# Hashed attention and an MLP on one core: the later queries of batch 0's first head group are hashed in a column-tiled matmul and their bits spread through DRAM, with the order of instructions rewritten

## The chip, the core and the metric

The kernel runs on 1 core of one Trainium2 chip. The metric is the device time in microseconds (us) of one execution; smaller is better. TensorE is called PE (its weight loads PEld), VectorE DVE, ScalarE ACT, GpSimd POOL and SyncE SP, as in the profile. SP's work is to issue most of the DMAs.

## What is computed

Four batches, 8 heads, 768 positions, head width 64. Queries and keys are hashed to 6 bits by the signs of a projection, and a query sees only the keys with the same 6 bits. The 8 heads side by side make rows of 512 for a normalised two-layer network with 2048 hidden units, which is added to its input.

```python
q_bits = (np.einsum('bhsd,dk->bhsk', q, proj) > 0).astype(np.int64)
k_bits = (np.einsum('bhsd,dk->bhsk', k, proj) > 0).astype(np.int64)
mask = q_bucket[:, :, :, None] == k_bucket[:, :, None, :]
scores = np.where(mask, scale * np.matmul(q, k.transpose(0, 1, 3, 2)), -1000000000.0)
attn = softmax(scores)                       # over the keys
x = heads_side_by_side(np.matmul(attn, v))   # (4, 768, 512)
xn = (x - mu) / np.sqrt(var + 1e-06) * g_ln
return x + np.maximum(xn @ w_ch1, 0.0) @ w_ch2
```

(The lines are shortened; `q_bucket` and `k_bucket` are the numbers that the bits spell.)

## The kernel before

**Tiling.** A batch's heads are two groups `g` of 4. Four heads lie in four strips of 32 partitions, so that a score matmul works on one strip and four of them fill the PE array. A unit `u` is 256 queries; there are 3 units in a batch and 12 in all. A step `s` is one unit, one group and one third `kp` of the keys: `s = 6u + 3g + kp`, 72 steps.

**A step.** `S` computes the scores of 4 heads: for each, three matmuls that add into one PSUM tile, the first on the bits (`G`, 6 partitions of a strip, values of plus or minus one half), the other two on the two halves of the head width. The bits' share is so scaled that a query and a key with unequal bits get a negligible weight. `E` is the exponential on ACT, in two halves of 2 heads. `A` multiplies by the values, with a column of ones for the row sums. `na` adds a very small multiple of the plain value sums, `nb` divides, `nc` and `ce` normalise the row, `rs` makes the inverse deviation, and `fl` transposes the row block by a DMA; for unit 0 PE transposes instead (`ft`) and DVE or ACT copies (`fc`). `F` and `R` are the first layer and its ReLU in eight parts, `D` the second layer in quarters for each half of the unit, `Z` the final addition, `O` the output's DMA.

**Inputs.** q and k come in as `X` tiles (`lx` in thirds for batch 0, `LX` whole for the others; four buffers, so a load waits for the last reader of the tile whose place it takes). DVE turns them in blocks of 32 (`tn` for batch 0, into three `tp` buffers; `tu` for the others), and `ca` or `CA` cast them to bf16 on ACT, DVE or POOL. `lv` and `cv` load and cast the values, `sv` and `sw` make batch 0's value sums with a matmul by ones. `lw1` and `lw2` load the network's weights in eight pieces by way of POOL's queue, and `lg` loads the row `g_ln` for all partitions.

**The hash.** For batch 0 there is one `ha` for each group, each of q and k and each third: two fp32 matmuls of 128 x 256, with a projection `pfull` that has the 6 columns of strip i at column 32i. So the six results of strip i land on the partitions where `G` wants them, and `bi` turns them to bits and writes them there. For batches 1 to 3, `hm` hashes a whole group in 16 instructions on 32 columns each, with `p32` (strip i's 6 columns at column 8i); four chunks of positions use the four column groups of the array at the same time. `bt` makes the bits in a tile `B`, and 16 small DMAs (`mo`) copy them to `G`, one for each chunk and strip.

**The order.** Nothing is scheduled at run time. A string `ORDER` holds words such as `ha.t.0.1.2`: the function, the engine (v DVE, a ACT, p POOL, s SP, t PE), and its numbers. Words are emitted in this order, and each engine runs its own words strictly in that order, waiting at each until its inputs and buffers are ready. For `tn`, `ca`, `ha` and `bi` the numbers are group, 0 for q or 1 for k, and third; for `S`, the step; for `F` and `R`, unit and part. SP issues its DMAs in order as well, all from one queue; the weights' DMAs have another.

The words of the front run over the first 60 us: hash, first ten steps, unit 0's network, and the loads of batch 1. Score steps 0 to 5 read queries 0 to 255 (third 0 of q); steps 6 to 11 read queries 256 to 511, steps 12 to 17 the rest. So the bits of group 0's thirds 1 and 2, which the change touches, are first read in step 6, 7 or 8. PSUM has the tags `scA` and `scB` (a half step's scores each), `acc` (the sums of `A`; lent to scores in steps 0 to 5), `f1` and `f2`.

Of the kernel before, what the change touches and what calls it, by code (L numbers as in the profile page):

```python
# [9 lines left out]
BF16 = mybir.dt.bfloat16  # L10
# [7 lines left out]
mem.v on.p.1 on.p.0 lp.a pf.v lx.s.0.1.1.3 tn.v.0.1.2 ca.p.0.1.2 tn.v.0.1.1 lx.s.0.0.0.1 tn.v.0.0.0 ca.a.0.0.0  # L18
ca.a.0.1.1 lx.s.1.0.0.1 warm.t ha.t.0.1.2 bi.v.0.1.2 tn.v.1.0.0 ca.p.1.0.0 ha.t.0.0.0 bi.v.0.0.0 lx.s.0.1.0.1
tn.v.0.1.0 ca.a.0.1.0 ha.t.1.0.0 bi.v.1.0.0 pmem.p p32.p S.t.2.2 E.a.2.1 E.a.2.0 lv.s.0.0.4 cv.p.0.0.2 ha.t.0.1.1  # L20
bi.v.0.1.1 ha.t.0.1.0 lx.s.1.1.0.3 tn.v.1.1.2 ca.p.1.1.2 S.t.1.2 E.a.1.1 E.a.1.0 lx.s.1.0.1.3 ha.t.1.1.2 bi.v.0.1.0
S.t.0.2 E.a.0.0 E.a.0.1 lg.s tn.v.1.1.1 ha.t.1.1.1 ca.p.1.1.1 bi.v.1.1.2 S.t.5.2 E.a.5.1 tn.v.1.1.0 ca.p.1.1.0
ha.t.1.1.0 cv.p.0.0.0 A.t.1.2 A.t.0.2 bi.v.1.1.1 lw1.p.0 E.a.5.0 S.t.4.2 E.a.4.1 lw1.p.1 lx.s.0.0.1.3 tn.v.0.0.2
tn.v.0.0.1 ha.t.0.0.1 ca.v.0.0.1 lw2.p.1 E.a.4.0 bi.v.1.1.0 sv.t.0 LX.s.1.0.1 tu.v.1.0.1.3 tu.v.1.0.1.1 tu.v.1.0.1.2
lw1.p.3 tu.v.1.0.1.0 lw2.p.0 CA.p.1.0.1.1 tn.v.1.0.2 A.t.2.2 bi.v.0.0.1 S.t.6.2 E.a.6.0 E.a.6.1 ha.t.1.0.2 sw.v.0
na.v.0.0 nb.v.0.0 S.t.3.2 nc.v.0.0 E.a.3.1 bi.v.1.0.2 ha.t.0.0.2 lv.s.0.4.4 cv.p.0.4.0 cv.p.0.4.2 sv.t.4 LX.s.1.0.0
tu.v.1.0.0.0 tu.v.1.0.0.2 lv.s.1.4.1 S.t.8.2 E.a.3.0 A.t.3.2 E.a.8.0 A.t.5.2 E.a.8.1 A.t.4.2 ca.v.1.0.2 tn.v.1.0.1
ca.v.1.0.1 bi.v.0.0.2 ha.t.1.0.1 S.t.7.2 E.a.7.1 E.a.7.0 LX.s.1.1.1 lw1.p.2 sw.v.4 na.v.0.1 nb.v.0.1 A.t.8.2
nc.v.0.1 A.t.6.2 ce.v.0.0 bi.v.1.0.1 ft.t.0.0 fc.a.0.0 S.t.10.2 E.a.10.0 E.a.10.1 ce.v.0.1 ft.t.0.1 rs.p.0
tu.v.1.0.0.1 A.t.7.2 fc.v.0.1 F.t.0.0 R.a.0.0 CA.v.1.0.0.0 LX.s.1.1.0 S.t.11.2 E.a.11.1 E.a.11.0 lw2.p.2  # L30
tu.v.1.0.0.3 CA.a.1.0.0.1 hm.t.1.0 bt.v.1.0 mo.s.1.0.3.0 mo.s.1.0.0.0 mo.s.1.0.2.3 mo.s.1.0.0.3 mo.s.1.0.1.2
mo.s.1.0.0.1 mo.s.1.0.1.3 mo.s.1.0.3.3 mo.s.1.0.0.2 F.t.0.7 R.v.0.7 lw2.p.3 S.t.9.2 E.a.9.1 CA.p.1.0.1.0 F.t.0.6
F.t.0.3 na.v.1.0 nb.v.1.0 A.t.10.2 ca.v.0.0.2 E.a.9.0 S.t.14.2 E.a.14.1 tu.v.1.1.0.3 A.t.9.2 R.v.0.6 mo.s.1.0.2.2
E.a.14.0 nc.v.1.0 R.v.0.3 lv.s.1.0.0 A.t.11.2 na.v.1.1 F.t.0.4 R.a.0.4 LX.s.2.1.1 F.t.0.1 R.a.0.1 S.t.13.2 E.a.13.0
E.a.13.1 nb.v.1.1 A.t.14.2 nc.v.1.1 ce.v.1.0 ce.v.1.1 fl.s.1.1 fl.s.1.0 F.t.0.5 R.a.0.5 tu.v.1.1.0.0 lv.s.1.4.2
F.t.0.2 R.a.0.2 LX.s.2.0.0 lv.s.1.4.3 lv.s.1.0.3 tu.v.1.1.0.1 mo.s.1.0.1.1 mo.s.1.0.1.0 mo.s.1.0.2.1 tu.v.1.1.1.3
S.t.12.2 E.a.12.1 E.a.12.0 tu.v.1.1.1.0 tu.v.1.1.0.2 CA.a.1.1.0.1 mo.s.1.0.2.0 lv.s.1.0.1 mo.s.1.0.3.1 LX.s.2.0.1
D.t.0.0.0 D.t.0.0.1 D.t.0.0.2 D.t.0.0.3 S.t.16.2 E.a.16.0 E.a.16.1 mo.s.1.0.3.2 tu.v.1.1.1.1 F.t.1.7 R.v.1.7
A.t.13.2 A.t.12.2 na.v.2.0 F.t.1.2 R.a.1.2 S.t.17.2 E.a.17.1 E.a.17.0 tu.v.1.1.1.2 CA.p.1.1.1.1 hm.t.1.1 Z.v.0.0
D.t.0.1.0 bt.v.1.1 mo.s.1.1.3.2 mo.s.1.1.3.0 mo.s.1.1.2.1 mo.s.1.1.1.1 mo.s.1.1.0.1 mo.s.1.1.0.0 mo.s.1.1.1.2  # L40
mo.s.1.1.3.1 F.t.1.0 R.a.1.0 S.t.15.2 E.a.15.0 E.a.15.1 rs.p.1 nb.v.2.0 nc.v.2.0 A.t.16.2 A.t.17.2 mo.s.1.1.0.3
# [78 lines left out]
def kernel(  # L120
# [15 lines left out]
    nc = tc.nc  # L136
    P = 128
# [453 lines left out]
```

## Time and profile before

| | |
|---|---|
| time, median of 3 runs (lowest to highest) | 304.76 us (303.95 to 304.84) |
| the profiled execution: time, span | 304.76 us, 303.0 us |
| mean granted PE clock in it | 0.998 |
| PE busy in the span | 292.2 us |
| ACT, DVE, POOL busy | 194.6, 169.7, 72.0 us |
| first score matmul, first `F` of unit 0, end of the last weight load on PE | 9.03, 35.67, 298.89 us |

The span is the time from the first to the last instruction of the execution. The profile's groups have, after the bar, the busy time of all, the mean ns of one, and the idle time of the engine before them with what ended it. fp32 matmuls have two records for each instruction, so one `ha` (two instructions) shows as four. In the chain and the timelines the first column is the start in us, the second the duration.

### The profile page before, as it was taken

Reading aid. Unit: us, or ns where it says so; the run is one execution under the profiler, and the core shown is the slowest. Engines: PE = TensorE matmul, PEld = TensorE weight load, DVE = VectorE, ACT = ScalarE, POOL = GpSimd, SP = SyncE. Lnnn points to the kernel's source line nnn. Section 1 sums busy time; section 2 is a strip of 40 time slices with the busy share of each in tenths; the row PEclk is TensorE's granted clock in tenths of the full one; section 3 lists DMA queues with packets and bytes.
Section 4 is the critical chain, followed back from the end, with each engine's and each line's share of the span. In section 5 each row is a group of like instructions: output and inputs, shape, how many; then the busy total and the mean of one; then the engine's idle time right before and its main releaser. Section 6 shows DMA issues by size and latency. Waiting matters only on the chain.

```text
span 303.0 us, 9838 instructions
## 1 busy us (share of the span) xinstructions
PE 292.2 (96%) x4319; PEld 204.8 (68%) x4360; DVE 169.7 (56%) x348; ACT 194.6 (64%) x215; POOL 72.0 (24%) x112
## 2 busy tenths in 40 slices
PE   8999899999999999999999999999999999999994
PEld 7667676676666667676667677776657667685673
DVE  4678878378258527766345767555217446266012
ACT  2977789667667788686567676557666767561320
POOL 2792500211771005041600520911000101001000
PEclk9999999999999999999999999999999999999999
DMA  6999996937255265516306100310502102403122
GB/s 202 381 340 306 209 205 142 268 111 169 47 147 122 61 217 167 94 74 160 73 2 175 38 8 8 75 42 19 89 2 71 37 2 19 105 4 74 30 71 69
DMA packets 30426, 33.58 MB, mean 111 GB/s; under 512 B 15536, under 2 KB 27056, under 8 KB 30384
## 3 DMA queue, kind: packets, MB, share of 16 engines
q1 hardware_dynamic: 25792, 28.50, 35.1%
q0 software_dynamic: 4224, 4.19, 8.4%
q8 instruction: 34, 0.56, 0.8%
q10 hardware_dynamic: 368, 0.26, 0.3%
q14 instruction: 8, 0.07, 0.1%
HBM read 27.53 MB, written 6.29 MB: 112 GB/s over the span
## 4 chain that ended last, share of the span: by engine, by line
PE 80%; DMA 6%; SPq 6%; DVE 3%; issue 2%; ACT 1%; DVEq 0%; ACTq 0%
PE f L511 26%; PE sc L443 15%; PE acc L458 10%; DMA X<-in_q_dram 4%; SPq L420 3%; PE hp L408 3%; DMA xnT<-xc 3%; ACT E L449 1%; SPq L294 1%; PE f_100None L527 1%; PE f_101None L527 1%; PE f L527 1%; PE f_11None L527 1%; PE f_51None L527 1%; PE f_80None L527 1%
## 5 line engine op out<-in xcount | busy, mean ns | idle before, releaser
L449 ACT ACTIVATE E<-sc,bias_sb 128x1024 bf16<-128x1024 f32 x144 | 153.1, 1111 | 49.5 <-PE sc L443 48.3
L511 PE MATMUL f<-xnT,w_sb 128*128 128x256 bf16 x768 | 99.3, 273 | 0.8 <-DMA xnT<-xc 0.7
L511 PEld LDWEIGHTS <-w_sb 128*128 128x128 bf16 x768 | 70.9, 98 | 23.5 <-issue 7.9
L519 ACT ACTIVATE hb<-f 128x512 bf16<-128x512 f32 x57 | 33.9, 597 | 44.6 <-PE f L511 44.5
L527 PEld LDWEIGHTS <-hb 128*128 128x128 bf16 x400 | 37.7, 98 | 34.5 <-issue 2.7
L521 DVE TENSOR_SCALAR hb<-f 128x512 bf16<-128x512 f32 x39 | 26.9, 690 | 46.7 <-PE f L511 46.4
L443 PE MATMUL sc<-qb,kb 32*128 32x256 bf16 x1152 | 52.2, 267 | 0.0
L458 PEld LDWEIGHTS <-E 128*128 128x128 bf16 x1152 | 40.0, 98 | 6.5 <-issue 3.8
L458 PE MATMUL acc<-vaug,E 128*128 128x65 bf16 x1152 | 43.4, 194 | 0.1
L443 PE MATMUL sc<-G 6*128 6x256 bf16 x576 | 41.7, 273 | 0.9 <-DVE G L249 0.3
L489 POOL TENSOR_SCALAR rs<-mv 128x2 f32<-128x2 f32 x12 | 7.1, 595 | 104.6 <-DVE mv L483 104.3
L443 PEld LDWEIGHTS <-kb 32*128 32x128 bf16 x1152 | 30.2, 93 | 1.6
L443 PEld LDWEIGHTS <-G 6*128 6x128 bf16 x576 | 15.2, 91 | 18.8 <-issue 15.6
L246 DVE STREAM_TRANSPOSE T<-X 128x384 f32<-128x384 f32 x48 | 24.8, 554 | 3.4 <-PE hp L408 1.4
L469 DVE SCALAR_TENSOR_TENSOR acc<-vsB,acc 128x520 f32<-128x520 f32 x24 | 16.8, 701 | 15.3 <-PE acc L458 15.0
L356 POOL TENSOR_TENSOR t<-vn 128x256 f32<-128x256 f32 x18 | 12.9, 727 | 35.0 <-DMA out_dram<-x 18.0
L346 POOL CAST vaug<-vn 128x768 bf16<-128x768 f32 x16 | 13.1, 831 | 25.9 <-DMA G<-B 12.7
L484 DVE SCALAR_TENSOR_TENSOR xc<-x,mv,gB 128x512 bf16<-128x512 f32 x24 | 18.6, 776 | 0.8
L480 DVE BATCH_NORM_STATS2 st<-x 128x6 f32<-128x256 f32 x48 | 18.0, 417 | 0.7
L476 DVE TENSOR_TENSOR x<-acc,rc 128x512 f32<-128x512 f32 x24 | 16.6, 691 | 0.8
L257 POOL CAST kb<-T 128x768 bf16<-128x768 f32 x10 | 8.4, 842 | 30.2 <-DVE T L246 30.2
L315 PE MATMUL hf<-tp,pfull 128*128 128x256 f32 x48 | 13.2, 401 | 0.6 <-DVE tp L246 0.5
(98 smaller groups left out, 223.8 us busy)
## 6 DMA issues: line engine op xcount, KB each, us to landing
out_dram<-x SPq DMA_DIRECT2D x44, 128.0 KB
X<-in_k_dram SPq DMA_DIRECT2D x7, 768.0 KB
X<-in_q_dram SPq DMA_DIRECT2D x6, 768.0 KB
vn<-in_v_dram SPq DMA_DIRECT2D x24, 192.0 KB
w_sb<-in_moe_w_ch_dram POOLq DMA_DIRECT2D x8, 512.0 KB, 16.5
vn<-in_v_dram SPq DMA_DIRECT2D x2, 768.0 KB
G<-B SPq DMA_DIRECT2D x96, 4.5 KB
X<-in_q_dram SPq DMA_DIRECT2D x2, 512.0 KB
```

The source lines that it names most:

```text
L246: nc.vector.transpose(d[:, j], s[:, j, kj0 : kj0 + n])
L443: nc.tensor.matmul(sc(s, i // 2)[:, i % 2, 256 * kk : 256 * kk + 256], lh, rh, start=(rep == 0), stop=(rep == 2), skip_group_check=True,)
L449: nc.scalar.activation(E(s)[:, heads(h)], sc(s, h), AF.Exp, scale=EXP_SCALE, bias=bias_sb)
L458: nc.tensor.matmul(acc[:, qt, (D + 1) * i : (D + 1) * (i + 1)], E(s)[:, i, 256 * kk + P * qt : 256 * kk + P * qt + P], vaug(u // 3)[:, 4 * ...
L469: nc.vector.scalar_tensor_tensor(acc, vs, EPS_ROW, acc, op0=AOP.mult, op1=AOP.add)
L476: nc.vector.tensor_tensor(xo, a[:, :, :, 0:D], rc.to_broadcast([P, 2, 4, D]), op=AOP.mult)
L480: nc.vector.bn_stats(stats(u)[:, qt, g], xt(u)[:, qt, 256 * g : 256 * g + 256])
L484: nc.vector.scalar_tensor_tensor(xc(u)[:, t], xt(u)[:, t], mv(u)[:, t, 0:1], gB, op0=AOP.subtract, op1=AOP.mult,)
L511: nc.tensor.matmul(f1[:, n].rearrange("p (t x) -> p t x", t=2), w1_sb[:, dt, P * nt : P * nt + P], xnT(u)[:, :, dt], start=(dt == 0), stop ...
L519: nc.scalar.activation(hb(u)[:, 2 * p : 2 * p + 2], f1, AF.Relu)
L521: eng.tensor_scalar_max(hb(u)[:, 2 * p : 2 * p + 2], f1, 0.0)
L527: nc.tensor.matmul(f2, hb(u)[:, nt, P * t : P * t + P], w2_sb[:, nt, half(h)], start=(nt == 0), stop=(nt == NNT - 1),)
```

## The change

`ha.t.0.0.1`, `ha.t.0.0.2` and their two `bi` go. In their place one `hq.t.0` hashes queries 256 to 767 of group 0 in 8 instructions on 32 columns and 128 positions each, four chunks in the four column groups, with `p32`. `bq` makes the bits in a tile of 128 x 128. `dw` writes this tile to a tensor in DRAM, and four `dr`, one for each strip, read it back into `G`. All five are DMAs from SP's queue; `dr` waits until `dw` has landed. The other hashes stay as they are.

The whole order is rewritten as well. In the front, the first load is third 0 of q instead of thirds 1 and 2 of k; `lg` stands behind the loads of batch 1's first tiles; `pmem` and `p32` come first on POOL; steps run 2, 1, 0, 5, 4, 3, 11, 10, 7, 6 instead of 2, 1, 0, 5, 4, 6, 3, 8, 7, 10; and the parts of `F` of each unit, the casts' engines and the DMAs stand in another sequence to the end of the kernel.

```diff
 ORDER = """
-mem.v on.p.1 on.p.0 lp.a pf.v lx.s.0.1.1.3 tn.v.0.1.2 ca.p.0.1.2 tn.v.0.1.1 lx.s.0.0.0.1 tn.v.0.0.0 ca.a.0.0.0
-ca.a.0.1.1 lx.s.1.0.0.1 warm.t ha.t.0.1.2 bi.v.0.1.2 tn.v.1.0.0 ca.p.1.0.0 ha.t.0.0.0 bi.v.0.0.0 lx.s.0.1.0.1
-tn.v.0.1.0 ca.a.0.1.0 ha.t.1.0.0 bi.v.1.0.0 pmem.p p32.p S.t.2.2 E.a.2.1 E.a.2.0 lv.s.0.0.4 cv.p.0.0.2 ha.t.0.1.1
-bi.v.0.1.1 ha.t.0.1.0 lx.s.1.1.0.3 tn.v.1.1.2 ca.p.1.1.2 S.t.1.2 E.a.1.1 E.a.1.0 lx.s.1.0.1.3 ha.t.1.1.2 bi.v.0.1.0
-S.t.0.2 E.a.0.0 E.a.0.1 lg.s tn.v.1.1.1 ha.t.1.1.1 ca.p.1.1.1 bi.v.1.1.2 S.t.5.2 E.a.5.1 tn.v.1.1.0 ca.p.1.1.0
-ha.t.1.1.0 cv.p.0.0.0 A.t.1.2 A.t.0.2 bi.v.1.1.1 lw1.p.0 E.a.5.0 S.t.4.2 E.a.4.1 lw1.p.1 lx.s.0.0.1.3 tn.v.0.0.2
-tn.v.0.0.1 ha.t.0.0.1 ca.v.0.0.1 lw2.p.1 E.a.4.0 bi.v.1.1.0 sv.t.0 LX.s.1.0.1 tu.v.1.0.1.3 tu.v.1.0.1.1 tu.v.1.0.1.2
-lw1.p.3 tu.v.1.0.1.0 lw2.p.0 CA.p.1.0.1.1 tn.v.1.0.2 A.t.2.2 bi.v.0.0.1 S.t.6.2 E.a.6.0 E.a.6.1 ha.t.1.0.2 sw.v.0
-na.v.0.0 nb.v.0.0 S.t.3.2 nc.v.0.0 E.a.3.1 bi.v.1.0.2 ha.t.0.0.2 lv.s.0.4.4 cv.p.0.4.0 cv.p.0.4.2 sv.t.4 LX.s.1.0.0
-tu.v.1.0.0.0 tu.v.1.0.0.2 lv.s.1.4.1 S.t.8.2 E.a.3.0 A.t.3.2 E.a.8.0 A.t.5.2 E.a.8.1 A.t.4.2 ca.v.1.0.2 tn.v.1.0.1
-ca.v.1.0.1 bi.v.0.0.2 ha.t.1.0.1 S.t.7.2 E.a.7.1 E.a.7.0 LX.s.1.1.1 lw1.p.2 sw.v.4 na.v.0.1 nb.v.0.1 A.t.8.2
...
-mo.s.1.0.0.1 mo.s.1.0.1.3 mo.s.1.0.3.3 mo.s.1.0.0.2 F.t.0.7 R.v.0.7 lw2.p.3 S.t.9.2 E.a.9.1 CA.p.1.0.1.0 F.t.0.6
-F.t.0.3 na.v.1.0 nb.v.1.0 A.t.10.2 ca.v.0.0.2 E.a.9.0 S.t.14.2 E.a.14.1 tu.v.1.1.0.3 A.t.9.2 R.v.0.6 mo.s.1.0.2.2
-E.a.14.0 nc.v.1.0 R.v.0.3 lv.s.1.0.0 A.t.11.2 na.v.1.1 F.t.0.4 R.a.0.4 LX.s.2.1.1 F.t.0.1 R.a.0.1 S.t.13.2 E.a.13.0
-E.a.13.1 nb.v.1.1 A.t.14.2 nc.v.1.1 ce.v.1.0 ce.v.1.1 fl.s.1.1 fl.s.1.0 F.t.0.5 R.a.0.5 tu.v.1.1.0.0 lv.s.1.4.2
-F.t.0.2 R.a.0.2 LX.s.2.0.0 lv.s.1.4.3 lv.s.1.0.3 tu.v.1.1.0.1 mo.s.1.0.1.1 mo.s.1.0.1.0 mo.s.1.0.2.1 tu.v.1.1.1.3
...
+on.p.0 mem.v warm.t pmem.p lp.a pf.v lx.s.0.0.0.1 tn.v.0.0.0 ca.a.0.0.0 ha.t.0.0.0 lx.s.0.1.1.3 tn.v.0.1.2
+ha.t.0.1.2 ca.a.0.1.2 tn.v.0.1.1 p32.p ca.p.0.1.1 bi.v.0.0.0 ha.t.0.1.1 on.p.2 lx.s.0.1.0.1 tn.v.0.1.0 ca.a.0.1.0
+bi.v.0.1.2 S.t.2.2 E.a.2.1 E.a.2.0 ha.t.0.1.0 bi.v.0.1.1 S.t.1.2 E.a.1.1 E.a.1.0 lx.s.1.0.0.1 tn.v.1.0.0 ca.v.1.0.0
+lx.s.1.1.0.3 tn.v.1.1.2 ha.t.1.1.2 tn.v.1.1.0 ca.p.1.1.2 ca.p.1.1.0 bi.v.0.1.0 ha.t.1.0.0 S.t.0.2 E.a.0.0 bi.v.1.1.2
+ha.t.1.1.0 bi.v.1.0.0 S.t.5.2 E.a.0.1 lv.s.0.0.4 cv.p.0.0.0 cv.p.0.0.2 lx.s.1.0.1.3 tn.v.1.0.1 ca.p.1.0.1 tn.v.1.1.1
+ca.p.1.1.1 ha.t.1.1.1 lx.s.0.0.1.3 tn.v.0.0.2 ca.p.0.0.2 bi.v.1.1.0 sv.t.0 E.a.5.1 A.t.1.2 A.t.0.2 A.t.2.2
+LX.s.1.0.0 tu.v.1.0.0.0 tn.v.0.0.1 bi.v.1.1.1 lw1.p.2 E.a.5.0 S.t.4.2 E.a.4.0 lv.s.0.4.4 cv.p.0.4.2 cv.p.0.4.0
+E.a.4.1 tu.v.1.0.0.1 sw.v.0 na.v.0.0 hq.t.0 nb.v.0.0 S.t.3.2 E.a.3.1 bq.v.0 ha.t.1.0.1 tn.v.1.0.2 ca.p.1.0.2
+tu.v.1.0.0.2 lw1.p.3 sv.t.4 LX.s.1.1.1 bi.v.1.0.1 S.t.11.2 nc.v.0.0 ca.p.0.0.1 E.a.3.0 A.t.3.2 A.t.4.2 A.t.5.2
+lw1.p.0 LX.s.1.0.1 tu.v.1.0.1.2 tu.v.1.0.1.3 lg.s E.a.11.0 E.a.11.1 S.t.10.2 E.a.10.1 E.a.10.0 lw2.p.1 sw.v.4
+na.v.0.1 nb.v.0.1 nc.v.0.1 ce.v.0.0 ce.v.0.1 rs.p.0 ha.t.1.0.2 bi.v.1.0.2 lw1.p.1 ft.t.0.0 fc.v.0.0 dw.s.0 dr.s.0.0
+dr.s.0.3 dr.s.0.1 dr.s.0.2 S.t.7.2 E.a.7.0 E.a.7.1 ft.t.0.1 fc.v.0.1 F.t.0.4 R.a.0.4 S.t.6.2 E.a.6.1 E.a.6.0
+tu.v.1.0.0.3 CA.a.1.0.0.1 tu.v.1.0.1.1 lw2.p.0 A.t.7.2 F.t.0.7 R.a.0.7 tu.v.1.0.1.0 hm.t.1.0 bt.v.1.0 mo.s.1.0.1.2
+mo.s.1.0.2.0 mo.s.1.0.3.2 CA.p.1.0.1.0 mo.s.1.0.2.2 mo.s.1.0.1.0 mo.s.1.0.1.1 mo.s.1.0.3.3 mo.s.1.0.2.3 S.t.8.2
+E.a.8.0 E.a.8.1 F.t.0.0 R.a.0.0 A.t.6.2 CA.p.1.0.1.1 tu.v.1.1.1.0 F.t.0.5 R.v.0.5 S.t.9.2 E.a.9.1 E.a.9.0
+mo.s.1.0.0.0 lv.s.1.4.3 lv.s.1.0.1 A.t.8.2 F.t.0.3 R.a.0.3 F.t.0.6 R.a.0.6 lw2.p.3 mo.s.1.0.0.3 mo.s.1.0.3.1 lw2.p.2
+mo.s.1.0.1.3 S.t.13.2 E.a.13.1 E.a.13.0 tu.v.1.1.1.3 LX.s.1.1.0 tu.v.1.1.1.2 na.v.1.0 nb.v.1.0 nc.v.1.0 A.t.9.2
+A.t.10.2 A.t.11.2 F.t.0.1 R.a.0.1 S.t.14.2 E.a.14.1 E.a.14.0 F.t.0.2 R.a.0.2 tu.v.1.1.1.1 na.v.1.1 nb.v.1.1 nc.v.1.1
+ce.v.1.1 A.t.13.2 fl.s.1.1 ce.v.1.0 fl.s.1.0 lv.s.1.4.1 D.t.0.0.0 LX.s.2.0.1 S.t.12.2 E.a.12.1 E.a.12.0 mo.s.1.0.2.1
...

+    def hq(eng, g):
+        hp = ps(f"hq{g}", [P, P], "f1")
+        for j in range(2):
+            for c in range(4):
+                nc.tensor.matmul(
+                    hp[32 * c : 32 * c + 32], p32[:, j], tp(g, 0, 1 + c // 2)[:, j, P * (c % 2) : P * (c % 2) + P],
+                    start=(j == 0), stop=(j == 1), skip_group_check=True,
+                )
+
     def Bq(g):
         return sb(f"Bq{g}", [P, P], BF16, "B", 2)
+
+    def bq(eng, g):
+        bits(Bq(g), made[f"hq{g}"])
+
+    def dw(eng, g):
+        made["hs", g] = dram.tile([4, 4, 8, P], BF16, name=f"hs{g}")
+        eng.dma_start(out=made["hs", g].rearrange("c i n w -> (c i n) w"), in_=Bq(g))
+
+    def dr(eng, g, i):
+        eng.dma_start(
+            out=Gt(0, g)[32 * i : 32 * i + NB, 0, 256:S].rearrange("n (c w) -> n c w", c=4),
+            in_=made["hs", g][:, i, :NB].rearrange("c n w -> n c w"),
+        )
```

## Prediction

> **What bounds the kernel now.** I read the page first: which engine is full, and the chain that ended last. The profiled execution took 304.76 us, its span 303.0 us; the 1.76 us around it I keep. 304.76 is also the median of the three runs. A kernel of this length can be told from no change at about 0.3%, 0.91 us.
>
> ```profile
> span 303.0 us, 9838 instructions
> PE 292.2 (96%) x4319; PEld 204.8 (68%) x4360; DVE 169.7 (56%) x348; ACT 194.6 (64%) x215; POOL 72.0 (24%) x112
> ...
> DMA  6999996937255265516306100310502102403122
> ...
> PE 80%; DMA 6%; SPq 6%; DVE 3%; issue 2%; ACT 1%; DVEq 0%; ACTq 0%
> ```
>
> PE is busy 96% and carries 80% of the chain, so work taken off PE is worth its time if PE then finds the next operands ready. The DMA row is full in its first seven slices (up to about 53 us): that is where the change puts its transfers. Next, the groups of the two hash forms and of the small loads in front of the scores:
>
> ```profile
> L315 PE MATMUL hf<-tp,pfull 128*128 128x256 f32 x48 | 13.2, 401 | 0.6 <-DVE tp L246 0.5
> L408 PE MATMUL hp<-T,p 128*32 128x192 f32 x192 | 9.0, 329 | 0.0
> L443 PEld LDWEIGHTS <-G 6*128 6x128 bf16 x576 | 15.2, 91 | 18.8 <-issue 15.6
> ```
>
> The first two give what is removed and the nearest relative of what is added. The third shows 15.6 us of "issue" ahead of the score loads: a score step (`S`) that follows an unsplit matmul starts late. In the timeline of PE, `F` lasts 0.79 us start to start, but 1.18 us with `S` behind it; `D` 0.76 and 1.17; `A` 0.49 and 0.69; `S` itself 0.77, `ha` 1.06, `hm` 1.44.
>
> Then the chain in order of time for the first 40 us, and SP's and POOL's timelines:
>
> ```profile
> 6.31 10.99 DMA X<-in_q_dram
> ...
> 17.40 1.44 DVE tp L246 x4
> ```
> ```profile
> 39.89 7.90 SPq L420 DMA_DIRECT2D G<-B  x10
> ```
> ```profile
> 16.98 1.79 POOL L330 DMA_DIRECT2D w_sb<-in_moe_w_ch_dram  x2
> ```
>
> The front is paced by the last piece of X (issued 6.31, used 17.40), because everything before it is in one queue; from there by DVE. The `G<-B` copies cost SP 0.79 us each. In the trace's packet records the first of these, issued 39.89, moves its first packet at 44.08, 4.2 us later, while the weight queue moves 200 packets of 1 KB per us; one issued near 47.1, when weights run out, starts at 48.4, after 1.3 us. The first weight load, issued 16.98, moves packets from 20.5.
>
> **The change, part by part.**
>
> Hash. `ha.0.0.1` and `ha.0.0.2` go: 2 x 1.06 = 2.12 us of PE. `hq` has 16 records of the column-tiled form with 128 columns; `hm` has 32 with 192 in 1.44 us. By count alone hq is 0.72, by count and columns 0.48; I take 0.60. Gain 1.5 us (1.4 to 1.64). DVE loses two bits steps of 0.41 and gains one of half their width, about 0.3: 0.5 us, at a place where DVE is full (3.79 and 3.93 busy of 4 us from 20 to 28), counted in the chain below.
>
> Order on PE. `S` after `D` rises from 10 to 14, after `A` falls from 10 to 9, after `F` stays 40; the cheap entries from `ha` or `hm` fall from 9 to 5, `hq` adds one. Adding all steps by what follows them, with the medians of such pairs, PE's program is 293.8 us before and 293.2 after: the hash gains 1.5, transitions give back 0.9.
>
> Start. The first load is now the query third (256 KB), then the keys. In this trace those 256 KB move in 1.0 us, so the keys, first used at 5.12, come at about 6.0. DVE then does two turns (1.4), a bits step (0.4), a turn (0.75) and the bits that `S.2` needs (0.4): first `S` at 9.4 instead of 9.03. PE waits 0.4 us there.
>
> Front up to `S.7`, the first step that reads the spread bits. gB's load (256 KB) now stands behind, so the last X piece comes about 1.0 us earlier, at 16.3. DVE from there: turn 0.75, bits 0.4, `tu` 0.55, turn 0.75, bits 0.4, `tu` 0.55, `sw` 0.4, `na` 0.7, `nb` 0.95, `bq` 0.3: `bq` ends near 22.1. PE runs `A.2` to 20.0, `S.4`, `hq` to 21.5, `S.3` at 22.0, `ha.1.0.1`, `sv.4`, `S.11` to about 25.3, where E.3 ends and `A.3 A.4 A.5` follow to 27.0. `S.10` and `ha.1.0.2` end at 29. `ft.0.0` needs `ce.0.0`: na 0.7, nb 0.95, nc 0.75, ce 0.98 behind A.5, at 30.6. So PE reaches `S.7` at 31.0 if the bits are there.
>
> What that is worth: from `S.7` on PE's steps sum to 266.9 us. Before, `S.10` started at 33.73 with a sum of 263.6 left, and 265.2 were needed (1.6 more in small waits). With the same 1.6, after would end its last weight load at 31.0 + 268.5 = 299.5 against 298.9: +0.6.
>
> The DRAM trip, the added wait. `dw` stands on SP behind LX.1.0.1 and gB, both issued by 19.8, so it leaves with bq at 22.1. Nearest rows: the last output write is issued at 300.08 and the span ends at 303.0, 2.9 us; the smallest read (prj) is issued at 0.79 and used at 2.54, 1.75 us. SP then waits for that write to land; mo, LX and the rest queue behind, none needed soon. Four `dr` at the 0.72 to 0.78 of `G<-B`. Low: 22.1 + 2.9 + 3 x 0.75 + 1.75 = 29.0, hidden below 31.0. High, with 4.2 us to the first packet both ways and about 0.5 to land: 22.1 + 4.7 + 2.25 + 4.7 = 33.8, a stall of 2.8. Which? Weight loads in between: POOL issues lw1.2 at about 20, but lw1.3, lw1.0, lw2.1 only after `ca.p.1.0.2` and `ca.p.0.0.1`, whose form took 1.52 us, so from 24.5 on, with packets 3.5 us later, at 28. The write escapes them, the last `dr` half so. I take 31.5, a stall of 0.5. All of PE's program queues behind it, so it counts in full.
>
> The Trainium skill ("DMA: Bandwidth & Descriptors", "Anatomy of one DMA") puts about 2.0 us of fixed time on a transfer; by it write and read would be in at 28.4, and the stall nothing. The same page ("Queues, rings and completion order") has each engine go round its queues packet by packet, which would not hold a small transfer behind weights; the 4.2 us above speak against it.
>
> Also, `ft.0.1` and `F.0.4` now stand next to each other with the copy `fc.0.1` (0.43) between; before, `A.7` lay there and PE still waited 0.32. +0.2.
>
> Later units. After a unit's last `ce`, the transposed copies need about 3.9 us to PE's first `F` (unit 9 had 3.9 and no wait). The sums leave 3.9 for unit 1 (5.0 before with a 0.36 wait, an LX load ahead in the queue), 3.7 for unit 9, 2.8 for unit 11 (3.0 before), 4.9 for unit 8, whose 0.35 wait may go. Net 0 (-0.4 to +1.0). The tail has the same steps: 0.
>
> Sum: 304.76 + 0.6 + 0.5 + 0.2 = 306.06; I say 306.0. Front's bounds: 31.0 may be 29.6 to 31.5; stall 0 to 2.8.
>
> **Rivals.**
>
> A, faster: the front gains more. The X piece comes 1.0 us earlier and two 1.06 us steps leave, and if `ce.0.0` comes at 29.2, S.7 starts at 29.6, with the bits at 29.0. PE ends at 29.6 + 268.5 = 298.1, 0.8 less than before, and unit 8's 0.35 goes too: 303.6. For it: DVE has 0.5 us less there. Against: A.3 to A.5 wait for E.3, and ACT has no less to do. It decides as soon as dr lands before `ce.0.0` and ce.0.0 before 29.8.
>
> B, much slower: the trip runs behind weights and late X loads. Bits at 33.8: 2.8 of stall instead of 0.5, 308.3. For it: the full DMA row and the 4.2 us. Against: POOL's weight loads are issued later than before.
>
> C, unit 1's transposed copies: they queue behind mo, lv and LX.1.1.0, while the last weight loads run. With unit 1's need of before, 5.35 against 3.9 of cover, it waits 1.4 instead of 0.36: 307.1.
>
> That the hash saves nothing on PE (hq as long as two ha) would add 1.5; `hm`'s rows exclude it.
>
> **How the numbers follow.** Forecast 0.44 (own range 305.0 to 307.0; 0.12 of it lies within 0.3%), A 0.32 (0.25 below 303.85, 0.07 within), B 0.16, C 0.08 (0.02 within). Faster 0.25, same 0.21, slower 0.54. The range reaches into A to 303.2 and past B to 308.4, leaving about 0.1 on either side.
>
> **What would show it.** hq rows near 0.5 to 0.7 us in all and no L315 pair for these queries; first score matmul near 9.4; a wait of PE at the scores of step 7, released by the DMA `G<-hs`, 0.5 us; the end of PE's last weight load near 300.1. If that wait is absent and F.0.4 starts before 32.5, A holds; if it is 2 us or more, B. Wrong altogether would be a PE wait above 1 us at a place that I don't name, or a front that is not paced by DVE.

## The result

| | before | after |
|---|---|---|
| time, median of 4 runs each (lowest to highest) | 304.8 us (303.95 to 305.42) | 312.89 us (312.65 to 313.8) |
| ratio after/before, 95% interval | | 1.0273 [1.024, 1.0306] |
| profiled execution: time, span | 304.76, 303.0 us | 313.06, 311.4 us |
| mean granted PE clock in it | 0.998 | 0.984 |
| `S.7`, the first step that reads the spread bits | | 34.34 us |
| end of the last weight load on PE | 298.89 us | 307.10 us |

The changed kernel is 2.7% slower, 8.1 us. Most of it is lost in the front, up to the hash of batch 1 (`hm.1.0`, 43.38 us); what is lost later is small beside it (below). A run more than 1.5% above the fastest of its kernel counts as slow and is left out of the ratios; in the experiments below these are two of e4's four runs, its profiled one among them, and one of e7's six.

### The profile after

From the page of after: the head, three rows of the 40 slices, and the shares of the chain of waits. `PE` and `PEclk` are in tenths of busy time and of the full clock.

```profile
span 311.4 us, 9865 instructions
PE 294.3 (95%) x4329; PEld 204.9 (66%) x4368; DVE 166.7 (54%) x342; ACT 198.1 (64%) x219; POOL 74.6 (24%) x113
...
PE   7998499999999989999999999999999999999994
PEclk9999579999999999999999999999999999999999
DMA  6999994791385931635731200130403100302122
...
PE 82%; DMA 8%; DVE 5%; issue 2%; SPq 1%; DVEq 0%
```

PE's row has one hole, the 4 in the fifth slice (31 to 39 us), and in that slice and the next the granted clock is 0.5 and 0.7. DMA has grown from 6% to 8% of the chain, and the DMA row is full just there.

The groups by line, then one from the groups by form:

```profile
L316 PE MATMUL hf<-tp,pfull 128*128 128x256 f32 x40 | 11.0, 401 | 0.7 <-DVE tp L247 0.5
L466 PE MATMUL sc<-G 6*128 6x256 bf16 x576 | 43.1, 276 | 5.2 <-DMA G<-hs 4.0
L466 PEld LDWEIGHTS <-G 6*128 6x128 bf16 x576 | 15.8, 92 | 24.5 <-issue 19.3
```
```profile
L328 PE MATMUL hq<-tp,p 128*32 128x128 f32 x16 | 0.6, 279 | 0.0
```

The hash is as cheap as forecast: 8 records of the old form less (13.2 to 11.0 us), 0.6 us for `hq`. The score matmuls now wait 4.0 us for the DMA `G<-hs`.

The chain in order of time (start, duration):

```profile
22.24 6.14 DMA hs<-Bq
...
28.40 0.32 SPq L344
...
30.31 5.54 DMA G<-hs
...
35.90 1.46 PE sc L466 x19
```

`bq` is done at 22.2. The write to DRAM takes 6.1 us, the four reads' issues run to 30.7, the last read lands 5.5 us after its issue began. In the packet records the write is issued at 22.24, has its first packet of 256 bytes at 26.17 and its last at 27.87; the reads are issued from 28.40, with packets from 32.51 to 35.40. So each half waits some 4 us before anything moves.

PE's timeline around it (start, duration, engine, line; in brackets the idle time before and what ended it):

```profile
30.72 0.40 PE L521 MATMUL ft<-ident,xc 128*128 128x128 bf16 x4 [0.98 <-DVE xc L507]
...
34.34 0.37 PE L466 MATMUL sc<-G 6*128 6x256 bf16 x1 [3.23 <-DMA G<-hs]
...
35.36 0.37 PE L466 MATMUL sc<-G 6*128 6x256 bf16 x1 [0.65 <-DMA G<-hs]
...
35.90 0.39 PE L466 MATMUL sc<-G 6*128 6x256 bf16 x2 [0.16 <-DMA G<-hs]
```

PE was ready for `S.7` at 31.1 (34.34 less the 3.23 of waiting); it has all bits at 35.9, 4.8 us later. And from then it is slow, as a table by stretches shows (from:to and length; PE, PEld, DVE, ACT, POOL busy, with instructions in brackets; granted clock; DMA share; GB/s). The DMA share is the time of all packets over that of 16 engines, so it can pass 1 where packets overlap.

```profile
28.00:31.00 3.00, 2.02 (x30) 1.30 (x22) 2.83 (x9) 2.12 (x2) 0.39 (x2) 1.00 1.08 145
31.00:34.30 3.30, 0.12 (x3) 0.00 (x0) 1.24 (x3) 0.00 (x0) 2.92 (x4) 0.67 1.19 189
34.30:37.30 3.00, 2.14 (x25) 0.89 (x26) 0.00 (x0) 0.10 (x1) 0.00 (x0) 0.50 1.24 197
37.30:40.20 2.90, 2.39 (x14) 1.42 (x13) 1.83 (x4) 2.02 (x2) 0.38 (x1) 0.50 1.24 207
40.20:43.40 3.20, 3.20 (x52) 2.30 (x51) 0.00 (x0) 2.25 (x3) 2.65 (x4) 0.66 0.78 111
```

The granted clock is 0.50 from 32.11 to 42.35, 10.24 us. In before it is full until PE's last matmul is over. From the last bits (35.9) to `hm.1.0` (43.38) this stretch takes 7.48 us.

Of what comes later, the largest piece is a wait for the transposed copy of unit 3, which before does not have:

```profile
111.25 1.03 PE L534 MATMUL f<-xnT,w_sb 128*128 128x256 bf16 x8 [1.02 <-DMA xnT<-xc]
```

Against it stand waits of 0.37 and 0.35 us for such copies in before, at units 1 and 8.

### The profile page after: what moved, and what is told of

Same layout as the page of the kernel before. It is cut to its first block, busy times and chain, and to the rows that moved or that the text cites. A ratio compares the mean times of both kernels' runs of the same rounds, so it can differ in the third digit from the quotient of the medians.

```text
span 311.4 us, 9865 instructions
## 1 busy us (share of the span) xinstructions
PE 294.3 (95%) x4329; PEld 204.9 (66%) x4368; DVE 166.7 (54%) x342; ACT 198.1 (64%) x219; POOL 74.6 (24%) x113
## 4 chain that ended last, share of the span: by engine, by line
PE 82%; DMA 8%; DVE 5%; issue 2%; SPq 1%; DVEq 0%
PE f L534 27%; PE sc L466 16%; PE acc L481 11%; DMA xnT<-xc 3%; PE hp L431 2%; DMA hs<-Bq 2%; DMA G<-hs 2%; PE hf L316 2%; DMA X<-in_k_dram 2%; PE f_101None L550 1%; PE f L550 1%; PE f_21None L550 1%; PE f_41None L550 1%; PE f_01None L550 1%; PE f_50None L550 1%
## 5 line engine op out<-in xcount | busy, mean ns | idle before, releaser
L534 PE MATMUL f<-xnT,w_sb 128*128 128x256 bf16 x768 | 100.5, 274 | 2.6 <-DMA xnT<-xc 1.2
L542 ACT ACTIVATE hb<-f 128x512 bf16<-128x512 f32 x60 | 35.7, 597 | 48.8 <-PE f L534 48.5
L544 DVE TENSOR_SCALAR hb<-f 128x512 bf16<-128x512 f32 x36 | 24.9, 691 | 53.6 <-PE f L534 53.2
L466 PE MATMUL sc<-qb,kb 32*128 32x256 bf16 x1152 | 53.6, 271 | 0.0
L466 PE MATMUL sc<-G 6*128 6x256 bf16 x576 | 43.1, 276 | 5.2 <-DMA G<-hs 4.0
L466 PEld LDWEIGHTS <-kb 32*128 32x128 bf16 x1152 | 30.7, 94 | 1.8
L258 POOL CAST kb<-T 128x768 bf16<-128x768 f32 x8 | 6.6, 826 | 44.5 <-DVE T L247 44.5
L316 PE MATMUL hf<-tp,pfull 128*128 128x256 f32 x40 | 11.0, 401 | 0.7 <-DVE tp L247 0.5
```

Source lines behind the costliest of these rows:

```text
L316: nc.tensor.matmul(hf(g, t, kp)[:, :256], pfull[:, j], tp(g, t, kp)[:, j], start=(j == 0), stop=(j == 1))
L466: nc.tensor.matmul(sc(s, i // 2)[:, i % 2, 256 * kk : 256 * kk + 256], lh, rh, start=(rep == 0), stop=(rep == 2), skip_group_check=True,)
L534: nc.tensor.matmul(f1[:, n].rearrange("p (t x) -> p t x", t=2), w1_sb[:, dt, P * nt : P * nt + P], xnT(u)[:, :, dt], start=(dt == 0), stop ...
L542: nc.scalar.activation(hb(u)[:, 2 * p : 2 * p + 2], f1, AF.Relu)
L544: eng.tensor_scalar_max(hb(u)[:, 2 * p : 2 * p + 2], f1, 0.0)
```

## The experiments

The runs carry the numbers e1 to e12. The theory to be tested: the trip through DRAM costs PE 4.8 us, because each half of it waits behind transfers already queued, and the pause halves PE's clock, which costs some 2 us more; the rest is the new order. The rivals: the pause is there but the order alone carries most of the loss; or the trip is slow by itself, whatever else the DMA engines carry; or SP's queue is what holds it. The edits below are words of `ORDER`; before ran beside each group of experiments, with medians of 304.42 to 305.3 us.

### The pause filled with matmuls that do nothing

48 (e1), then 110 (e5) matmuls of 128 x 128 on a tile of ones stand between `ft.0.0` and `S.7`. They add work that no output needs.

```diff
-ha.t.1.0.2 bi.v.1.0.2 lw1.p.1 ft.t.0.0 fc.v.0.0 dw.s.0
+ha.t.1.0.2 bi.v.1.0.2 lw1.p.1 ft.t.0.0 fill.t.48 fc.v.0.0 dw.s.0
```

> The changed kernel with 48 dummy matmuls (ones by ones into the idle acc bank) on PE between ft.0.0 and S.7; 46 of them took 4.3 us at the start, so they fill the wait from 31.0 to about 35.4. Theory: besides the wait itself (bits complete at 35.9 instead of 31.0, 4.9 us) the halved clock from 32.1 to 42.3 costs 2.5 us; with PE kept busy the clock stays at 1.0, hm.1.0 starts at about 40.9 instead of 43.4, and the time falls by 2 to 3 us, to 310 to 311. Rival: the wait alone is the loss and the clock record means little; then the time stays at 312.9 or grows by up to 0.5.

Measured: 316.88 us, 1.0396 [1.0363, 1.0429]. PE's timeline:

```profile
31.89 2.84 PE L293 MATMUL fill<-ones 128*128 128x128 bf16 x48
...
36.75 0.28 PE L469 MATMUL sc<-G 6*128 6x256 bf16 x2 [0.66 <-DMA G<-hs]
```

The 48 took 2.8 us, too short for a pause that lasted to 36.75 here; the clock was still halved from 37.82 to 44.65. So this run decided nothing on the clock. It shows something else: the later work slid behind unit 1's transposed copy, and PE waited 2.9 us there, with a second halving from 65.13.

```diff
-ha.t.1.0.2 bi.v.1.0.2 lw1.p.1 ft.t.0.0 fc.v.0.0 dw.s.0
+ha.t.1.0.2 bi.v.1.0.2 lw1.p.1 ft.t.0.0 fill.t.110 fc.v.0.0 dw.s.0
```

> As the kernel with 48 dummy matmuls, but with 110: there 48 took 2.7 us, not 4.4, ended at 34.6 while the bits came until 36.3, and the clock still dropped. 110 take 6.2 us, from 31 to about 37.2, past the bits. Theory (wait 4.9 plus halved clock 2.5): the clock stays at 1.0 through this stretch, and from S.7 to hm.1.0 PE needs about 5.5 us instead of the 9.1 of the changed kernel; hm.1.0 starts near 42.7 although S.7 starts at 37.2. Rival (the stretch after S.7 is slow for other reasons): S.7 to hm.1.0 still takes 8 us or more, hm.1.0 near 45.5. The time itself also holds unit 1's wait, which moved from run to run; 312 to 316.

Measured: 312.55 us, 1.0217 [1.0163, 1.0271]. The stretches of the filling and of what follows it:

```profile
31.70:38.00 6.30, 6.30 (x114) 6.23 (x112) 1.38 (x3) 0.04 (x1) 3.04 (x4) 1.00 1.18 189
38.00:43.40 5.40, 4.77 (x90) 3.40 (x92) 1.83 (x4) 4.04 (x5) 2.26 (x3) 1.00 1.06 176
```

The filling lasts 2 us longer than the pause, to 38.0, and the clock stays at 1.00. From there `S.7` to `hm.1.0` takes 5.29 us instead of the 7.48 us of after: the halved clock costs 2.2 us (or a little more, since five of the 24 matmuls of `S.7` were done before 35.9 in after). The filler spends that gain again: `hm.1.0` starts at 43.32 against 43.38, and the whole time can't be told from that of after. This is the clearest evidence for the clock's share.

### The old hash in the new order (e2)

```diff
-na.v.0.0 hq.t.0 nb.v.0.0 S.t.3.2 E.a.3.1 bq.v.0 ha.t.1.0.1
+na.v.0.0 ha.t.0.0.1 ha.t.0.0.2 nb.v.0.0 S.t.3.2 E.a.3.1 bi.v.0.0.1 bi.v.0.0.2 ha.t.1.0.1
 ...
-fc.v.0.0 dw.s.0 dr.s.0.0 dr.s.0.3 dr.s.0.1 dr.s.0.2 S.t.7.2
+fc.v.0.0 S.t.7.2
```

> The changed kernel's order with the old hash in it: two ha where hq stood, two bi where bq stood, no dw and no dr. Theory: all of the loss comes from the DRAM trip, and the order by itself costs about what the prediction said without the trip: S.7 starts near 31.5, the clock stays full, 305.5 to 306.5 us. Rival: the rewritten order itself loses most of it (other waits, more entries into split matmuls): 309 to 313.

Measured: 306.22 us over 10 runs, 1.005 [1.0026, 1.0073]: 1.5 us above before (0.8 to 2.2). PE's timeline:

```profile
22.98 0.29 PE L464 MATMUL sc<-G 6*128 6x256 bf16 x4
...
31.42 0.40 PE L519 MATMUL ft<-ident,xc 128*128 128x128 bf16 x4 [0.97 <-DVE xc L505]
...
31.75 0.29 PE L464 MATMUL sc<-G 6*128 6x256 bf16 x4
```

The first of these lines is `S.3`, to which the text comes back at the end. `S.7` now follows `ft.0.0` with no wait. So of the 8.1 us 1.5 belong to the rewritten order, and the other 6.6 to what the new hash gains and its trip costs together; the rival that the order carries the loss falls.

### What holds the trip: the weights, gB, or SP's queue

Five of the eight weight loads moved behind `rs.0` (e3):

```diff
-tu.v.1.0.0.2 lw1.p.3 sv.t.4 ... A.t.5.2 lw1.p.0 LX.s.1.0.1 ... E.a.10.0 lw2.p.1 sw.v.4 ... rs.p.0 ha.t.1.0.2
+tu.v.1.0.0.2 sv.t.4 ... A.t.5.2 LX.s.1.0.1 ... E.a.10.0 sw.v.4 ... rs.p.0 lw1.p.3 lw1.p.0 lw1.p.1 lw2.p.1 lw2.p.0 ha.t.1.0.2
```

> The changed kernel with five of the weight loads (lw1.3, lw1.0, lw1.1, lw2.1, lw2.0) moved on POOL behind rs.0, so that their packets start near 35. Theory: the trip is long because of traffic ahead of it (first packets 3.9 and 4.1 us after the issues); without the weights dw starts at about 24.5 and lands by 26, dr is in by 30 to 31, S.7 starts at about 31 and the clock stays full; F.0.7 then waits for lw1.3 until 38 to 39, and the time is 306 to 309. Rival: the trip takes about 6 us each way by itself (write receipt and read), S.7 still starts at 34 or later, 311 to 314.

Measured: 311.52 us, 1.0212 [1.0136, 1.0289], from two runs only (309.76 and 313.28). SP's timeline (`SPq`: issuing; xN: so many DMAs):

```profile
23.29 0.33 SPq L339 DMA_DIRECT2D hs<-Bq  x1
...
29.62 1.33 SPq L342 DMA_DIRECT2D G<-hs  x4
```

The write still takes 6.3 us, with its first packet at 27.69: gB and one weight load were ahead of it. But the reads are through at once: issued in 1.3 us instead of 2.3, first packet 0.9 us after the first issue, last packet at 31.85. `S.7` starts at 32.09 without a wait. What was won is lost later: `F.0.7` waits 1.15 us for its weights, to 38.96, the clock is halved for 3.41 us twice, and PE waits 3.3 us in all for transposed copies.

`lg`, the load of gB (the row `g_ln`), alone moved ahead of batch 1's tiles (e4):

```diff
-lx.s.1.0.1.3 tn.v.1.0.1 ... tu.v.1.0.1.3 lg.s E.a.11.0
+lx.s.1.0.1.3 lg.s tn.v.1.0.1 ... tu.v.1.0.1.3 E.a.11.0
```

> The changed kernel with gB's load moved from directly ahead of dw to its place of before, among the first loads. Theory: dw's first packet (26.2) stood behind gB's packets (22.3 to 25.5); it now comes at about 23.7, all bits 2.3 us earlier, and if the gap is then too short for the clock to drop the gain is up to 4.8: 308 to 310.6. Rival: the weights alone hold dw back, and gB's place changes nothing: 312.5 to 313.5.

Measured: 312.53 us (308.29 to 314.45); the ratio, 1.0165 [1.0088, 1.0243], rests on two runs (308.29 and 311.87), which scatter too widely for a finer reading. In the trace, that of the run of 313.19, the write's first packet comes 2.3 us after its issue instead of 3.9, but the packets then go on until 28.29, and the first read is issued 5.7 us after the write. The last packet of the reads comes at 35.29, against 35.40 in after. So in this trace gB's place alone does not shorten the trip; the time alone does not settle it.

Both together, with six weight loads behind `rs.0` (e9):

```diff
-lx.s.1.0.1.3 tn.v.1.0.1 ... lw1.p.2 ... lw1.p.3 ... lw1.p.0 ... lg.s ... lw2.p.1 ... rs.p.0 ha.t.1.0.2 bi.v.1.0.2 lw1.p.1 ... lw2.p.0
+lx.s.1.0.1.3 lg.s tn.v.1.0.1 ... rs.p.0 lw1.p.2 lw1.p.3 lw1.p.0 lw1.p.1 lw2.p.1 lw2.p.0 ha.t.1.0.2 bi.v.1.0.2
```

> The changed kernel with gB's load among the first loads and six weight loads behind rs.0. With gB early alone, the write's first packet came 2.3 us after its issue instead of 3.9, but it landed only 0.5 us sooner; with the weights later alone, the read half became fast (first packet 0.9 us after issue, all bits 2.7 us after the first issue), the write half stayed at 6.3. Theory (both halves are held by what is ahead of them: gB and the X tiles, then the weights): the write starts 1.3 to 2 us after its issue and lands within 3 to 4 us, all bits by 29 to 30, PE reaches S.7 without a wait, the clock stays at 1.0; F.0.4 and F.0.7 then wait for their weights, 306 to 310 in all. Rival (a write to DRAM takes 6 us here whatever the traffic): first dr again 6 us after dw.

Measured: 313.7 us, 1.0299 [1.0248, 1.035]. SP's timeline and the largest new wait:

```profile
22.93 0.33 SPq L339 DMA_DIRECT2D hs<-Bq  x1
...
25.73 1.33 SPq L342 DMA_DIRECT2D G<-hs  x4
```
```profile
PE f L532 <- DMA w_sb<-in_moe_w_ch_dram: 5.5, 1, 5.5
```

Now the first packet comes 0.8 us after the issue, the first read can be issued after 2.8 us, and the last packet of the reads comes at 28.88: from the write's issue to that packet the trip takes 6.0 us instead of 13.2. So it is not slow by itself; the transfers in front of it make it so. PE has the bits at `S.7` without a wait, and then stands 5.5 us at `F.0.4` for its weights, with the clock halved from 34.27 to 44.51. Here the pause has only changed its name, but not because the DMA engines had no room. By stretches:

```profile
28.90:34.30 5.40, 2.88 (x46) 1.74 (x36) 5.15 (x13) 4.01 (x4) 2.86 (x4) 1.00 0.00 0
34.30:38.30 4.00, 0.00 (x0) 0.00 (x0) 0.42 (x1) 0.23 (x1) 4.00 (x7) 0.50 1.09 167
```

After the reads the engines stood still for 5.4 us, since the weights waited on POOL behind `rs.0`. An order that issues the weights right behind the reads, but ahead of `rs.0`, was not tried; whether it keeps both gains stays open.

The write issued from ACT's queue (e10):

```diff
-nb.v.0.0 S.t.3.2 E.a.3.1 bq.v.0 ha.t.1.0.1 ... fc.v.0.0 dw.s.0 dr.s.0.0
+nb.v.0.0 bq.v.0 dw.a.0 S.t.3.2 E.a.3.1 ha.t.1.0.1 ... fc.v.0.0 dr.s.0.0
```

> The changed kernel with dw alone issued by ACT, whose queue holds nothing else then. It leaves about 1 us later, behind E.4.1. Theory A (the write waits in SP's queue behind gB and X tiles): the first packet comes within 1.5 us of the issue and dr starts at 26 to 27 instead of 28.4; with the bits about 2 us sooner 309 to 311. Theory B (it is the DMA engines that are full, whichever queue): again 4 to 6 us to landing, dr at 28.5 or later, 312 to 314.

Measured: 312.64 us, 1.0256 [1.0196, 1.0315], as after. ACT's timeline, then SP's:

```profile
22.99 0.35 ACTq L339 DMA_DIRECT2D hs<-Bq  x1
```
```profile
29.06 2.26 SPq L342 DMA_DIRECT2D G<-hs  x4
```

In a queue with nothing of its own ahead, the write still moves its first packet only 3.3 us after the issue, and the first read can be issued after 6.1 us. ACT's queue is not slow by itself: the load of the projection, issued from it at 0.79 us on idle engines, has its first packet at 1.80. So it is not SP's queue that holds the write; what is left is the load on the 16 DMA engines (share 1.16 from 23.0 to 26.3 us). The Trainium skill ("DMA: Bandwidth & Descriptors", "Queues, rings and completion order") says that SP's and ACT's queues are rings on the same 16 engines, and this run agrees. By its round robin, packet by packet, one would look for this write early. Its packets do run in between those of weights and gB once they begin; in what order the engines take the rest first, so that it waits 3.3 us, these runs don't show.

### Other work over the trip

If the trip can't be made shorter, other work may stand over it (e6). `S.9`, `A.11`, `A.10`, `A.9`, `ft.0.1`, `F.0.4`, `F.0.7` and `hm.1.0` go ahead of `S.7`, and unit 1's group 1 is normalised before its group 0:

```diff
-ft.t.0.0 fc.v.0.0 dw.s.0 ... dr.s.0.2 S.t.7.2 E.a.7.0 E.a.7.1 ft.t.0.1 fc.v.0.1 F.t.0.4 R.a.0.4 S.t.6.2 ... A.t.7.2 F.t.0.7 R.a.0.7 ... hm.t.1.0
+ft.t.0.0 S.t.9.2 E.a.9.1 E.a.9.0 fc.v.0.0 ft.t.0.1 fc.v.0.1 dw.s.0 ... dr.s.0.2 A.t.11.2 A.t.10.2 F.t.0.4 R.a.0.4 ... A.t.9.2 F.t.0.7 R.a.0.7 na.v.1.1 nb.v.1.1 hm.t.1.0
 ...
+S.t.7.2 E.a.7.0 E.a.7.1 ... F.t.0.0 R.a.0.0 ... S.t.6.2 E.a.6.1 E.a.6.0 ... A.t.7.2 F.t.0.5 R.v.0.5 S.t.8.2 E.a.8.0 E.a.8.1 ... A.t.6.2 F.t.0.3 R.a.0.3 F.t.0.6 R.a.0.6 ... A.t.8.2
```

> The changed kernel with the DRAM trip left as it is, but with PE work that needs none of its bits put into the wait: S.9, ft.0.1, A.11, A.10, A.9, F.0.4, F.0.7 and hm.1.0 stand ahead of S.7 (unit 1's second group before its first). Theory: the trip costs only what PE has not to do meanwhile; PE reaches S.7 at 37 with the bits there at 36, the clock stays full, and 304.5 to 306 us remain. Rival: DVE and ACT can't keep up with that order, or the weights are not there yet, and PE waits at other steps: 308 or more.

Measured: 309.74 us, 1.0137 [1.009, 1.0185]. The last packet of the reads comes at 35.93, `S.7` starts at 37.70 and does not wait for them, and the clock stays full. By the ratios half of the loss comes back (from 2.7% to 1.4%). Two other waits take their place:

```profile
PE sc L464 <- ACT E L470: 3.0, 5, 0.8
```
```profile
PE f L532 <- DMA xnT<-xc: 3.3, 3, 1.8
```

Steps 7, 6 and 8 now stand so close that ACT's exponentials can't follow (3.0 us in 5 places), and the transposed copies come late. The longest wait for a copy:

```profile
107.64 1.03 PE L532 MATMUL f<-xnT,w_sb 128*128 128x256 bf16 x8 [1.79 <-DMA xnT<-xc]
```

This is unit 3's first `F`; the other two are those of units 5 and 7 (0.79 and 0.74 us). At unit 1 PE does not wait in this run.

Against the second wait, the load `LX.1.1.0` moved behind unit 1's copies (e7). By the line above it could not help: none of the 3.3 us lies at unit 1, nor does the 1.0 us of after that the expectation names.

```diff
-tu.v.1.1.1.3 LX.s.1.1.0 tu.v.1.1.1.2 ... fl.s.1.0 lv.s.1.4.1
+tu.v.1.1.1.3 tu.v.1.1.1.2 ... fl.s.1.0 LX.s.1.1.0 lv.s.1.4.1
```

> The kernel with the wait covered, and with LX.1.1.0 (768 KB) moved behind unit 1's two transposes on SP. Theory: these transposes stood behind that load and PE waited 1.0 us for them in the changed kernel and 2.9 with the dummy matmuls; now they land earlier and the wait goes: 0.5 to 1.5 us less than the covered kernel, 303.5 to 305. Rival: the wait is due to the cover of 3.9 us alone; no difference.

Measured: 315.88 us, 1.0344 [1.0305, 1.0383]. Worse, and units 3 and 5 still wait 1.87 and 0.84 us for their copies. DVE's own order has a turn (`tu`) of that tile soon after and stands 7.5 us at it; a ReLU queued behind on DVE comes late, and PE waits 4.8 us for it, with the clock halved from 62.58 to 69.41:

```profile
PE f L532 <- DVE hb L542: 4.8, 1, 4.8
```

The same order with the old hash (e8; the hash's edit as above):

> The same order as the kernel with LX.1.1.0 moved, but with the old hash in it (two ha, two bi, no dw, no dr): it measures what hq is worth once its trip is hidden. Theory: hq took 0.4 us on PE against 2.1 for two ha, so the old hash is 1.0 to 1.7 us slower than its twin. Rival: PE waits for DVE at this place anyway (S.3 waited for nb.0.0), and the two are equal within 0.3.

Measured: 315.18 us, 1.0338 [1.029, 1.0385]. It has the same wait (4.6 us), and the two hashes can't be told apart: the intervals of the ratios nearly coincide.

Against the first wait, the steps of e6 spaced two parts of `F` apart (e11). One ReLU (`R.0.3`) also goes from ACT to DVE, and the halves of `E.6` change places:

```diff
-F.t.0.0 R.a.0.0 CA.p.1.0.1.1 S.t.6.2 ... A.t.7.2 F.t.0.5 R.v.0.5 S.t.8.2 ... A.t.6.2 F.t.0.3 R.a.0.3 F.t.0.6
+F.t.0.0 R.a.0.0 F.t.0.5 R.v.0.5 CA.p.1.0.1.1 S.t.6.2 ... A.t.7.2 F.t.0.3 R.v.0.3 S.t.8.2 ... A.t.6.2 F.t.0.6
```

> The covered kernel with S.7, S.6 and S.8 two F steps apart instead of one. There PE waited 3.0 us in five places for E on ACT, since each step's scores need both score banks and a step's E takes 2.2 us. Theory: the three waits around S.6 and S.8 (0.2, 0.7, 0.8) go, 1.2 to 1.8 us less than the covered kernel, 307.5 to 308.5. Rival: they move to the next S; no difference.

Measured: 307.17 us over 10 runs, 1.0079 [1.0053, 1.0106]; the clock full, no wait for transposed copies, 2.2 us of waits for `E` left. So the spacing took 0.8 us off the waits that it was meant for; the larger part of the gain on e6, 3.3 us in the traces, is the copies' waits, which it was not meant for. This is the best version that keeps the new hash, 2.4 us above before by its ratio. No version tried beats before.

Its order with the old hash (e12):

> The order with the wait covered and the S steps spaced (307.17 us with the new hash), but with the old hash in it: two ha, two bi, no dw and no dr. Here the trip is hidden and the clock full in the twin, so the difference is what the new hash is worth by itself. The prediction took 1.5 us for it (2.12 for two ha less 0.60). Theory: PE waits for ce.0.0 at ft.0.0 in either case, where ft.0.0 came 0.6 us earlier after the first S with the new hash than with the old; so 0.3 to 0.9 us slower than 307.17. Rival: the full 1.2 to 1.7 us, since PE carries the chain. Second rival: the old hash is faster, because the five DMAs of the trip hold up others.

Measured: 307.77 us over 10 runs, 1.0094 [1.006, 1.0129]. This pair sets the two hashes beside each other where the trip is hidden. The times don't tell them apart: the ratios differ by 0.0015, about 0.5 us for the new one, with intervals that overlap; and the two runs belong to different groups, in which before itself took 304.42 and 305.30 us, so that the medians less before's say the opposite (2.75 and 2.47 us). In the profiles `ft.0.0` comes 21.3 us after the first `S` with the new hash and 21.9 with the old, and the same in after against e2. So up to `ft.0.0` the new hash is worth 0.6 us, not the 1.5 us that its instructions add up to; in the whole time no gain of it is shown.

## Why the prediction was wrong

**The step that failed is the term of the DRAM trip**, "I take 31.5, a stall of 0.5". It measured 35.9 and 4.8 us, beyond even the high end of 33.8. Two things in it were mis-sized. The wait for a first packet was 3.9 us in the write and 4.1 us in the read, near the 4.2 of the row from before that the high end used, but the value taken lay far below it: the write was said to escape the weights, and it stood behind gB, X tiles and the first weight load (e3, e4, e9). That load, `lw1.2`, the prediction itself has issued at about 20, and by its own 3.5 us to the packets (20.73 less 16.98 in before is rather 3.75) it would have been on the engines from 23.5, in the middle of the write; only the later loads were counted, from 28. In after its packets begin at 23.89, and weights run with hardly a break until 49. Then, packets once begun were taken to be through in half a microsecond; among the others' packets they spread over 1.7 us in the write and 2.9 in the four reads. The issues of the four reads were no part of it: 1.9 us from the first start to the last, against 2.25. The low end, 6.9 us for the whole trip, is near what it takes on engines that are nearly free: 6.0 in e9, 2.8 of them until the reads can be issued. The 2.0 us of fixed time cited beside it stand in a part of the page on GpSimd's path, while these DMAs go by SP.

**A second term was missing**: the halved clock behind the pause, 2.2 us (e5). The trace of before had no pause of that kind and so no row for it; the prediction put it at nothing without a reason.

**The sum by the runs**: 4.8 for the wait, 2.2 for the clock, and 0.9 for the rewritten order net of the hash (1.5 by e2, less the 0.6 by which `ft.0.0` comes sooner) make 7.9 of the 8.1 measured; with nothing for the hash it is 8.5. The 1.5 has an interval of 0.8 to 2.2, so the agreement is no closer than that. The prediction's 0.6 + 0.2 for that last part, with the hash in it, was about right, in part by luck: it puts the later units at nothing, and unit 3 waited 1.0 us.

**The front was right**: first `S` at 9.40 (9.4 said), `bq` from 21.93 to 22.21 (22.1), `ft.0.0` at 30.72 (30.6), `hq` 0.6 us. It was a little more right than its sums: the terms listed for the first `S` end at 9.0 (6.0 + 2.95), those for `ce.0.0` at 30.4 (27.0 + 3.38).

What that front meant for the hash was not followed through. The forecast goes by the chain up to `S.7`, but the gain of the hash is still given as 1.5 us, and a hash that saves nothing as 1.5 us more. In the runs part of the time taken off PE turns into a wait. With the new hash `S.3` waits for DVE's `nb.0.0`:

```profile
22.07 0.49 PE L466 MATMUL sc<-G 6*128 6x256 bf16 x4 [0.48 <-DVE x L499]
```

In e2 `S.3` starts at 22.98 without a wait (the line is above). So `S.3` comes 0.9 us sooner, not 1.5, and `ft.0.0` 0.7 us sooner; 0.1 us of that is the first `S`.

**The rivals**: B has the mechanism, a trip behind weights and late X loads; its price of 2.8 us was too low for the reasons above, and it has no clock in it. Its argument against, that POOL's loads are issued later than before, did not help: while the reads waited, the DMA engines moved 189 GB/s, and in the packet records all of that is weights. A's first condition, bits before `ce.0.0`, occurred only in e9 (28.88), and there the weights took the gain; `ce.0.0` itself was never there before 29.8. C did not occur in after (0.17 us at unit 1's copies), but it came in e1 and e3 (2.89 and 2.04 us), and with 0.62 us in e2. Later units, for which the prediction allowed up to 1.0 us, waited 1.02 us in after, at unit 3.

## What to carry to other kernels

A small DMA in front of waiting work costs what is queued on the DMA engines ahead of it, not its own size: where the DMA row is full, price each hop by the slowest first packet in the trace, count a trip through DRAM twice, and add the spread of its packets. Whatever wait that leaves on PE, ask whether it drops the clock, because the work behind it is then slow as well. And credit work taken off an engine only up to the next place where that engine waits for another (here `S.3`).

## What the runs showed of the hardware

**The clock falls without an idle gap of a window's length.** All halved stretches that end before the program does last multiples of 3.41 us (10.24 in after, 6.83 in e1, 3.41 in e3). The Trainium skill ("TensorE: Matmul & The Clock Gate", "Part 1: The HAM clock gate") has such a free-running window of about 3.4 us, and says that PE falls to half clock after an idle one. The length agrees; the condition here is milder. In e2, two windows in turn:

```profile
30.03:33.44 3.41, 1.97 (x34) 1.12 (x34) 3.20 (x10) 2.39 (x3) 1.78 (x3) 1.00 1.20 195
33.44:36.85 3.41, 3.30 (x35) 1.87 (x35) 1.46 (x4) 1.90 (x3) 3.13 (x5) 0.50 1.20 171
```

PE was busy 1.97 of 3.41 us, 58%, its longest gap 0.97 us, and the next window was granted half. In after, the window from 28.70 to 32.11, with 1.44 us busy, came ahead of the halving. In e3 one with 2.13 us (62%) did:

```profile
30.33:33.74 3.41, 2.13 (x35) 1.17 (x34) 3.15 (x9) 2.30 (x3) 1.75 (x3) 1.00 0.03 7
```

But no bound on the busy share comes out of these runs. Windows with no more than that were followed by the full clock, as in e4, two windows ahead of its halving:

```profile
28.50:31.91 3.41, 1.97 (x26) 1.23 (x25) 2.97 (x7) 2.17 (x3) 0.73 (x1) 1.00 1.17 160
31.91:35.33 3.42, 0.74 (x6) 0.35 (x6) 3.13 (x8) 0.00 (x0) 1.49 (x3) 1.00 1.24 200
```

In e8 a window with 1.88 us (55%) was followed by the full clock too. The same 1.97 us stood ahead of half in e2 and of full here. So something other than the busy time of a window decides near 60%, and these runs don't show what.

**Latency under load.** The same write of 32 KB to DRAM had its first packet 0.8 us after its issue, and the reads that wait for it could be issued after 2.8 us, with no weights and no gB ahead of it (e9); it was 3.9 and 6.1 us with them (after), and 3.3 and 6.1 us from ACT's queue (e10).
